# A pair of key chunks gets its maximum from one chunk's scores and a positive score difference, with seven PSUM banks split 4 + 3

## The chip, the core and the metric

The kernel runs on one core of one Trainium2 chip. Its time is the device time of a run in microseconds (us); lower is better. The engines named below are PE (TensorE, the matrix multiplier; PEld is its weight load), DVE (VectorE), ACT (ScalarE), POOL (GpSimd) and SP (SyncE, which issues most transfers). PSUM, where PE writes its results, has eight banks of 128 x 512 float32.

## The reference

Two attention blocks over the same input, each with its own weights, mixed by a gate. There are 2048 tokens, 512 channels and 32 heads of 16 channels, so 64 heads in all.

```python
def _A_ref(x, wqkv, wo):                      # _B_ref is the same
    qkv = ((x @ wqkv).reshape(B, S, 3, H, Dh)).transpose(2, 0, 3, 1, 4)
    q, k, v = qkv[0], qkv[1], qkv[2]
    scores = jnp.einsum("bhqd,bhkd->bhqk", q, k) * (Dh ** -0.5)
    p = _softmax(scores, axis=-1)
    o = jnp.einsum("bhqk,bhkd->bhqd", p, v)
    return o.transpose(0, 2, 1, 3).reshape(B, S, D) @ wo

g = _sigmoid((x * gate_w).sum(-1, keepdims=True))
return g * a + (1 - g) * b
```

The softmax needs, for each query, the maximum of its scores over all 2048 keys.

## The kernel before

**Layout.** q and k are split in two parts each (a rounded one and the rest) and stacked along the rows, 48 rows for a head (`q_st`, `k_st`, three buffers each, one for a head), so that one matmul of 48 rows gives nearly exact float32 scores. The stack stands twice, at rows 0 and 64 (`HALVES`), and `rows()` takes the two in turn, so that two such matmuls run side by side. Two more rows hold the negative maximum of each query.

**Two products for each score.** For a block of 128 queries (a round `m`; 16 rounds are a head, `NT`), `max_product` multiplies the block with the four chunks of 512 keys, and DVE reduces the results over the keys to a maximum. Later, `score` multiplies in the other orientation (128 keys by 512 queries), with the maximum already subtracted by the two added rows; ACT takes exp from PSUM into `p`. `attend` multiplies `p` with V into the bank `acc`, four 32-column groups of PE side by side.

**Loop.** After a prologue (projections of q, k and v, and the maxima of the first 20 rounds, `run_ahead`) the main loop does two rounds a step: eight `score` products for rounds r and r+1, eight products to the maximum for the rounds 20 ahead, and the V product of the rounds before. I call such a step a pair. The engines work through their own queues in order, and the order is written by hand in the string `FULL`, one letter a step: "e" is a `score` with its exp, "m", "A", "B", "x" are the products to the maximum in their order (chunks 0 to 3 of the first round, then of the second), and a digit n stands for `attend_next(n)`, the V product of n quarters (of 128 queries) of a round, four quarters a round. Output projections that are due go in front of the first digit. `LATE` serves the last 10 pairs, whose maxima are all done.

**PSUM and the maximum.** Chunks 0 and 1 go to one bank each out of two (`ps_m1`), chunks 2 and 3 to a double bank (`ps_m2`), which DVE reduces in one go (128x1024). Chunk 1 of the second round of a pair ("x") isn't reduced by DVE directly: ACT copies it to SBUF, POOL takes the maximum of its two halves in three operations (subtract; clamp to at least 0; add), and DVE reduces the remaining 256 columns ("y", a pair later). This is not done for the last block of a head. Three partial maxima a block go to `mxp`; `max_split` joins them once a head, and `max_rows` transposes them (DVE) and sends them through DRAM into the stacks of q. `ps_st` has three banks for the scores, and `acc` one.

**A pool's buffers** are handed out in turn: a product that takes a buffer waits until the last reader of that buffer's former content is done.

Of the kernel before, what the change touches and what calls it, by code (L numbers as in the profile page):

```python
# [51 lines left out]
def gated_mha(ctx: ExitStack, tc: tile.TileContext, xT, x, wqkv_a, wo_a, wqkv_b, wo_b, gate_w, out):  # L52
# [12 lines left out]
    kd = [[dram.tile([2, HG, DH, S], F32, name=f"kd{s}{g}") for g in range(NG)] for s in range(2)]  # L65
    vd = [dram.tile([S, H * 17], F32, name=f"vd{s}") for s in range(2)]
    od = [dram.tile([HG, NQ, 32, 512], F32, name=f"od{g}") for g in range(2 * NG)]
    md = [dram.tile([2, S], F32, name=f"md{i}") for i in range(3)]
# [1 line left out]

    ident = const.tile([P, P], BF, name="ident")
    make_identity(nc, ident)
    q_st, k_st = [], []

    def new_stack(tp):
        i = len(q_st)
# [2 lines left out]
        for b in HALVES:  # L79
            pool.memset(k_st[i][b + 32:b + 64, :].bitcast(F32), -1.0)  # L80

    for _ in range(2):
        new_stack(const)


    def load_stacks(h, halves=HALVES):
# [4 lines left out]
        qs, ks = qd[s][g], kd[s][g]  # L91

        def pairs(t, step):
            v = t[0, j]
            return bass.AP(tensor=v.tensor, offset=v.offset, ap=[[S, DH], [step, 2], [1, S]])
# [11 lines left out]
    PARTS = ((0,), (1,), (2, 3))  # L107
    mxp = {}
    turn = [0]
    banks_m, halved = {}, []  # L110

    def rows():
        turn[0] ^= 1
        return HALVES[1 - turn[0]]

    def max_product(m, c, fold=False):
        h, t = divmod(m, NT)
        if t == 0 and c == 0:
            mxp[h] = small.tile([P, NT, 3], F32, name="mxp")
        q, k = q_st[h % 3], k_st[h % 3]  # L120
        part = min(c, 2)
        if c < 3:
            n = len(PARTS[part])
            banks_m[m] = (ps_m1 if n == 1 else ps_m2).tile([P, n * 512], F32, name=f"ps_m{n}")
        ps = banks_m[m]
        b = rows()
        o = max(0, c - 2) * 512
        pe.matmul(ps[:, o:o + 512], q[b:b + SC, t * P:(t + 1) * P], k[b:b + SC, c * 512:(c + 1) * 512],  # L128
                  start=True, stop=True)
        if fold:  # L130
            x = small.tile([P, 512], F32, name="fold", bufs=2)
            d = x[:, :256]
            act.copy(x, ps)  # L133
            pool.tensor_tensor(d, d, x[:, 256:], op=ALU.subtract)  # L134
            pool.tensor_scalar(d, d, 3.4028234e38, 0.0, op0=ALU.min, op1=ALU.max)  # L135
            pool.tensor_tensor(d, d, x[:, 256:], op=ALU.add)  # L136
            halved.append((mxp[h][:, t, part:part + 1], d))
        elif c != 2:
            dve.tensor_reduce(mxp[h][:, t, part:part + 1], ps, op=ALU.max, axis=AX.X)  # L139

    def max_part(m, part):
        for c in PARTS[part]:
            max_product(m, c)

    def max_halved():
        o, d = halved.pop(0)
        dve.tensor_reduce(o, d, op=ALU.max, axis=AX.X)  # L147

    mparts = {}

    def max_split(h):
        halves = mxp.pop(h)
        m = small.tile([P, NT], F32, name="mrow")
        mp = small.tile([P, 2, NT], F32R, name="mparts")
        dve.tensor_reduce(m, halves, op=ALU.max, axis=AX.X)  # L157
# [25 lines left out]
    with tc.tile_pool(name="xs", bufs=1) as xs, tc.tile_pool(name="pro", bufs=2) as pro, \  # L183
# [34 lines left out]
        def project_qk(s, g, isk, between):  # L218
            hi, lo = wblocks.pop((s, isk * DM + g * P))
            dst = (kd if isk else qd)[s][g]  # L220
            for half in range(2):
                ps = ps_pro.tile([P, 1024], F32, name="ps_pro")
                for c in range(2):
                    cc = half * 2 + c
                    n = 0
                    for a, b in ((hi, xh[cc]), (lo, xh[cc]), (hi, xl[cc])):
                        for k in range(KC):
                            pe.matmul(ps[:, c * 512:(c + 1) * 512], a[:, k], b[:, k],  # L228
                                      start=n == 0, stop=n == 3 * KC - 1)
                            n += 1  # L230
                pt = [pro.tile([P, 1024], F32R, name=f"part{i}") for i in range(2)]
                act.copy(pt[0], ps)  # L232
                dve.tensor_tensor(pt[1], ps, pt[0].bitcast(F32), op=ALU.subtract)  # L233
                for i in range(2):
                    nc.sync.dma_start(dst[i].rearrange("h d t -> (h d) t")[:, half * 1024:(half + 1) * 1024],
                                      pt[i].bitcast(F32))
                between()

        v_st = [const.tile([P, H, 17], F32, name=f"v_st{i}") for i in range(2)]
# [3 lines left out]
        def project_v(s, t):  # L243
            hi, lo = wblocks[s, 2 * DM]
            c, o = divmod(t * P, 512)
            last = s == 1 and t == NT - 1
            ps = ps_m1.tile([P, 512], F32, name="ps_m1") if last else ps_pro.tile([P, 1024], F32, name="ps_pro")
# [24 lines left out]
        ahead = [(m, part) for m in range(NT + LEAD) for part in range(3)]  # L272

        def run_ahead(n):
            turn[0] = 0
            for _ in range(n):
                m, part = ahead.pop(0)
                max_part(m, part)
                if (m, part) == (NT - 1, 2):
# [20 lines left out]
        for t in range(NT):  # L300
            project_v(1, t)
            if pending:
                pending[0] += 1
                if pending[0] == 3:
                    max_rows(pending.pop() - 3)
            if t and t != NT - 2:
                run_ahead(3)
# [120 lines left out]
    banks, fill_only = [], []  # L428

    def result_bank():  # L430
        banks.append(len(banks) % 5)
        if banks[-1] % 2 or not fill_only:
            return ps_m1.tile([P, 512], F32, name="ps_m1")
        return ps_st.tile([P, 512], F32, name="ps_st")

    def project_out(side, t):
# [118 lines left out]
    def attend(r, qa, qb):  # L555
# [13 lines left out]
        if final and last:  # L569
            ev = work.tile([P, 512], F32, name="ev")  # L570
            act.copy(ev, acc)
            hi = work.tile([P, 512], F32R, name="ev_hi")
# [33 lines left out]

    FULL = "eem4emeAeB2emex2AyeB"
    LATE = "ee2ee2ee2ee2"  # L610
    after = {}

    for r in range(0, ROUNDS, 2):
# [8 lines left out]
        if kt == 0 and h + 2 < NH:  # L622
            load_stacks(h + 2)
        m = r + NT + LEAD
        scored = parts = 0
        waiting = len(halved)
        for step in FULL if m < ROUNDS else LATE:
            if step == "e":
                score(r + scored // 4, scored % 4)
                scored += 1  # L630
            elif step in "mABx":
                mm, c = m + parts // 4, parts % 4
                max_product(mm, c, step == "x" and mm % NT != NT - 1)
                parts += 1
            elif step == "y":
                if waiting:
                    max_halved()
            else:
                for a in projects:
                    project_out(*a)  # L640
# [39 lines left out]
```

## Time and profile before

| | |
|---|---|
| Median of 3 runs | 2844.58 us (2844.14 to 2844.75) |
| Profiled execution, span | 2843.0 us |
| Main loop, first exp to end | about 295 to 2812 us |
| Busy share in 900 to 1000 us | PE 98.4%, DVE 95.9%, ACT 95.7%, POOL 35.3% |
| Granted clock of PE there | 1.00 |

The busy share of an engine is the time in which at least one of its instructions is under way; instructions of one engine overlap a little, so the time from one start to the next tells more than the length of one. An entry "[0.42 <-DVE mxp L139]" is idle time of the engine before the instruction and what ended it. In a group's row stand its count, busy time, mean length in ns, and the idle time in front with its releasers.

### The profile page before, as it was taken

To read this page: it belongs to the slowest core of one execution; us is meant where nothing else is said; L and a number is where in the kernel's file an instruction comes from. 1 tells how busy PE (TensorE), PEld (TensorE's weight loads), DVE (VectorE), ACT (ScalarE), POOL (GpSimd) and SP (SyncE) were. 2 spreads that over 40 slices of the span, in tenths; PEclk is the share of its full clock that TensorE was granted. 3 is DMA by queue.
4 is the path that set the end of the run, shared out by engine and by line. 5 is a ranking of instruction groups with operands and counts; after the bars stand their busy time and mean duration, and the time that the engine had idled before them with its cause. 6 is when DMAs were issued, how large, how long until landed. Compare 5 with 4: busy or idle time off the path is not lost.

```text
span 2843.0 us, 56787 instructions
## 1 busy us (share of the span) xinstructions
PE 2795.6 (98%) x22168; PEld 1230.1 (43%) x22168; DVE 2464.7 (87%) x3367; ACT 2412.5 (85%) x4696; POOL 1042.4 (37%) x1686
## 2 busy tenths in 40 slices
PE   8999999999999999999999999999999999999999
PEld 6877433333333333333333444433333333334445
DVE  3135899999999999999999988899999999998884
ACT  3221799999999999999999877899999999998785
POOL 1000355453433333333433555333333344345431
PEclk9999999999999999999999999999999999999999
DMA  6673333222332222232432342232222233233302
GB/s 237 203 229 122 82 69 78 58 52 54 66 58 55 55 43 58 52 56 54 85 54 52 92 94 62 54 56 51 60 43 56 54 70 70 54 72 80 76 6 91
DMA packets 83747, 214.30 MB, mean 75 GB/s; under 512 B 21878, under 2 KB 32086, under 8 KB 70934
## 3 DMA queue, kind: packets, MB, share of 16 engines
q1 hardware_dynamic: 80918, 201.76, 31.2%
q0 software_dynamic: 2560, 8.91, 1.3%
q8 instruction: 174, 2.85, 0.4%
q14 instruction: 95, 0.78, 0.1%
HBM read 145.87 MB, written 64.74 MB: 74 GB/s over the span
## 4 chain that ended last, share of the span: by engine, by line
PE 74%; DVE 16%; ACT 8%; issue 2%; DMA 0%; SPq 0%; ACTq 0%
PE acc L563 28%; PE ps_st L602 22%; DVE mxp L139 14%; PE ps_m L128 12%; PE ps_pro L228 6%; ACT p L604 5%; PE ps_m L445 3%; PE ps_pro L251 3%; ACT ev L580 1%; ACT fold L133 1%; DVE mxp L147 1%; DMA raw<-in_xT 0%; DVE mrow L157 0%; PE ps_st L445 0%; DVE rn L400 0%
## 5 line engine op out<-in xcount | busy, mean ns | idle before, releaser
L139 DVE TENSOR_REDUCE mxp<-ps_m 128x1 f32<-128x512 f32 (+1 forms) x2633 | 2190.3, 890 | 135.1 <-PE ps_m L128 61.0
L604 ACT ACTIVATE p<-ps_st 128x512 f32<-128x512 f32 x4096 | 2153.5, 610 | 177.0 <-PE ps_m L128 100.5
L128 PE MATMUL ps_m<-k_st,q_st 48*128 48x512 f32 x4096 | 1407.2, 441 | 5.3 <-DVE mxp L139 0.8
L602 PE MATMUL ps_st<-q_st,k_st 50*128 50x512 f32 x4096 | 1379.8, 438 | 0.0
L563 PE MATMUL acc<-p,vg 128*17 128x256 f32 (+1 forms) x12360 | 1182.8, 455 | 29.5 <-ACT ev L580 28.0
L602 PEld LDWEIGHTS ps_st<-q_st,k_st 50*128 50x128 f32 x4096 | 662.1, 184 | 801.6 <-ACT p L604 748.0
L128 PEld LDWEIGHTS ps_m<-k_st,q_st 48*128 48x128 f32 x4096 | 677.1, 184 | 251.8 <-DVE mxp L139 233.0
L134 POOL TENSOR_TENSOR fold<-fold 128x256 f32<-128x256 f32 x439 | 321.1, 731 | 1096.5 <-ACT fold L133 1096.5
L563 PEld LDWEIGHTS acc<-p,vg 128*17 128x17 f32 x12360 | 205.3, 95 | 466.3 <-issue 414.6
L136 POOL TENSOR_TENSOR fold<-fold 128x256 f32<-128x256 f32 x439 | 322.1, 734 | 36.6
L133 ACT COPY fold<-ps_m 128x512 f32<-128x512 f32 x439 | 261.3, 595 | 0.0
L135 POOL TENSOR_SCALAR fold<-fold 128x256 f32<-128x256 f32 x439 | 175.6, 400 | 38.5
L147 DVE TENSOR_REDUCE mxp<-fold 128x1 f32<-128x256 f32 x439 | 179.5, 409 | 0.0
L158 POOL CAST mparts<-mrow 128x16 fp32r<-128x16 f32 x64 | 12.6, 197 | 401.0 <-DVE mrow L157 401.0
L232 ACT CAST part<-ps_pro 128x1024 fp32r<-128x1024 f32 x32 | 32.5, 1015 | 132.9 <-PE ps_pro L228 132.9
L233 DVE TENSOR_TENSOR part<-ps_pro,part 128x1024 fp32r<-128x1024 f32 x32 | 39.2, 1225 | 111.4 <-ACT part L232 111.4
L445 PE MATMUL ps_m<-wo,ot 128*128 128x512 f32 (+1 forms) x354 | 90.9, 401 | 0.0
L254 ACT COPY v_st<-ps_pro 128x512 f32<-128x512 f32 x31 | 18.2, 587 | 77.4 <-PE ps_pro L251 77.4
L228 PE MATMUL ps_pro<-xh,whi 128*128 128x512 f32 x256 | 73.0, 404 | 8.8 <-ACT xh L214 8.7
L180 POOL DMA_DIRECT2D vg<-vd x32 | 25.6, 799 | 137.5 <-DMA vd<-v_st 137.1
L445 PEld LDWEIGHTS ps_m<-wo,ot 128*128 128x128 f32 (+1 forms) x354 | 63.9, 188 | 21.3 <-ACT fold L133 7.0
L228 PE MATMUL ps_pro<-xh,wlo 128*128 128x512 f32 x256 | 69.7, 395 | 0.0
(94 smaller groups left out, 822.1 us busy)
## 6 DMA issues: line engine op xcount, KB each, us to landing
k_st<-kd SPq DMA_DIRECT2D x128, 256.0 KB
q_st<-qd SPq DMA_DIRECT2D x128, 256.0 KB
qd<-part SPq DMA_DIRECT2D x32, 512.0 KB
kd<-part SPq DMA_DIRECT2D x32, 512.0 KB
k_st<-kd SPq DMA_DIRECT2D x128, 128.0 KB
q_st<-qd SPq DMA_DIRECT2D x128, 128.0 KB
od<-ev SPq DMA_DIRECT2D x63, 256.0 KB
vd<-v_st SPq DMA_DIRECT2D x32, 272.0 KB
```

The source lines that it names most:

```text
L128: pe.matmul(ps[:, o:o + 512], q[b:b + SC, t * P:(t + 1) * P], k[b:b + SC, c * 512:(c + 1) * 512], start=True, stop=True)
L133: act.copy(x, ps)
L134: pool.tensor_tensor(d, d, x[:, 256:], op=ALU.subtract)
L135: pool.tensor_scalar(d, d, 3.4028234e38, 0.0, op0=ALU.min, op1=ALU.max)
L136: pool.tensor_tensor(d, d, x[:, 256:], op=ALU.add)
L139: dve.tensor_reduce(mxp[h][:, t, part:part + 1], ps, op=ALU.max, axis=AX.X)
L147: dve.tensor_reduce(o, d, op=ALU.max, axis=AX.X)
L228: pe.matmul(ps[:, c * 512:(c + 1) * 512], a[:, k], b[:, k], start=n == 0, stop=n == 3 * KC - 1)
L445: pe.matmul(ps, ot[a][:n, slot, sl], wt[b][:n, g], start=G == groups[0] and i == 0, stop=G == groups[-1] and i == 2)
L563: pe.matmul(acc[32 * c:32 * c + 17, qa * P:qb * P], v[:, 4 * a + c if final else kt, j], p[:, c * 512 + qa * P:c * 512 + qb * P], start=fi ...
L602: pe.matmul(ps, k[b:b + SC + 2, kk * P:(kk + 1) * P], q[b:b + SC + 2, cc * 512:(cc + 1) * 512], start=True, stop=True)
L604: act.activation(pt[r][:, c * 512:(c + 1) * 512], ps, AF.Exp, scale=SCALE)
```

## The change

A maximum of two chunks is taken as max(s0, s1) = s0 + max(s1 - s0, 0). Since scores are linear in k, s1 - s0 is the product of q with the difference of the two key chunks. The prologue makes that difference for each head (`rise_k`: one DVE and three POOL operations in each of eight blocks, and two more writes to DRAM), `load_stacks` loads it into `x_st` (48 rows by 512; two more loads a head).

For the first round of each pair (from the first pair whose products can be made ahead) chunks 0 and 1 are then done in two steps. "D" (`max_rise`), a pair earlier: a product with `x_st`, and ACT writes its positive part (Relu) to SBUF. "A" (`max_pair`): a product with chunk 0, and one DVE operation adds the positive part and takes the maximum over the 512 columns. All other chunks are plain 512-column reductions ("m", `max_plain`): six a pair. ACT's copies, POOL's halving and the double bank are gone; `mxp` has four columns a block, the unused one preset to the lowest number by POOL. The number of PE products is the same. `ps_m` has three banks for all products to the maximum, and `ps_st` four. The order of a pair is new, and the V product is cut 3, 3 and 2 quarters instead of 4, 2 and 2; the second 3 is the last quarter of one round and two of the next.

```diff
-    ps_m1 = ctx.enter_context(tc.tile_pool(name="ps_m1", bufs=2, space=PSUM))
-    ps_m2 = ctx.enter_context(tc.tile_pool(name="ps_m2", bufs=1, space=PSUM))
+    ps_m = ctx.enter_context(tc.tile_pool(name="ps_m", bufs=3, space=PSUM))
...
+        if h and halves[-1] == HALVES[1]:
+            x = x_st[h % 2]
+            dma(x[:32].bitcast(F32), pairs(xs, HG * DH * 512, 512))
+            dma(x[32:SC].bitcast(F32), xs[0, j])
...
-    def max_product(m, c, fold=False):
+    def scores_bank(m, c):
         h, t = divmod(m, NT)
...
+        ps = ps_m.tile([P, 512], F32, name="ps_m")
         b = rows()
...
+        pe.matmul(ps, q[b:b + SC, t * P:(t + 1) * P], k, start=True, stop=True)
+        return ps, mxp[h][:, t]
+
+    def max_plain(m, c):
+        ps, o = scores_bank(m, c)
+        dve.tensor_reduce(o[:, c:c + 1], ps, op=ALU.max, axis=AX.X)
...
+    def max_rise(m):
+        ps, _ = scores_bank(m, "rise")
+        rises[m] = small.tile([P, 512], F32, name="rise")
+        act.activation(rises[m], ps, AF.Relu)
+
+    def max_pair(m):
+        ps, o = scores_bank(m, 0)
+        rise = rises.pop(m)
+        dve.tensor_tensor_reduce(out=rise, in0=ps, in1=rise, scale=1.0, scalar=LOWEST,
+                                 op0=ALU.add, op1=ALU.max, accum_out=o[:, 0:1])
...
+                if isk and half == 0:
+                    d = pro.tile([P, 512], F32, name="rise_k", bufs=1)
+                    dve.tensor_tensor(d, ps[:, 512:], pt[0][:, :512].bitcast(F32), op=ALU.subtract)
+                    pool.tensor_tensor(d, d, pt[1][:, :512].bitcast(F32), op=ALU.subtract)
+                    dt = [pro.tile([P, 512], F32R, name=f"rise_p{i}", bufs=1) for i in range(2)]
+                    pool.tensor_copy(dt[0], d)
+                    pool.tensor_tensor(dt[1], d, dt[0].bitcast(F32), op=ALU.subtract)
+                    for i in range(2):
+                        nc.sync.dma_start(xd[s][g][i].rearrange("h d t -> (h d) t"), dt[i].bitcast(F32))
...
-            project_qk(s, g, isk, lambda: run_ahead((i >= 10) + (i >= 13)))
+            project_qk(s, g, isk, run_ahead if i >= 10 else lambda: None)
...
-    ps_st = ctx.enter_context(tc.tile_pool(name="ps_st", bufs=3, space=PSUM))
+    ps_st = ctx.enter_context(tc.tile_pool(name="ps_st", bufs=4, space=PSUM))
...
-    FULL = "eem4emeAeB2emex2AyeB"
-    LATE = "ee2ee2ee2ee2"
+    FULL = "m3memeem3meAe2Dmeee"
+    LATE = "e2ee2ee2ee2e"
...
+            elif step == "m":
+                max_plain(*plain.pop(0))
+            elif step == "D":
+                if m + 2 < ROUNDS:
+                    max_rise(m + 2)
+            elif step == "A":
+                if m in rises:
+                    max_pair(m)
+                else:
+                    max_plain(m, 0)
+                    max_plain(m, 1)
```

**PE's queue.** One pair in the middle of a head before, from its 512-column V product on (`ps_m` is the maximum's bank, of either kind; `[waits ...]` names the engine whose progress the instruction waits for):

```order
L563 MATMUL acc<-p,vg 17x512 x4
L602 MATMUL ps_st<-q_st_2010,k_st_2011 128x512 [waits Activation_49]
L128 MATMUL ps_m_12733<-k_st_114,q_st_113 128x512
L602 MATMUL ps_st<-q_st_2010,k_st_2011 128x512 [waits Activation_49]
L128 MATMUL ps_m_12739<-k_st_114,q_st_113 128x512 [waits DVE_49]
L602 MATMUL ps_st<-q_st_2010,k_st_2011 128x512 [waits Activation_49]
L128 MATMUL ps_m_12739<-k_st_114,q_st_113 128x512
L563 MATMUL acc<-p,vg 17x256 x4
```

The same place after the change, from "D" of one pair to the second V product of the next:

```order
L135 MATMUL ps_m<-x_st_127,q_st_123 128x512 [waits DVE_49]
L135 MATMUL ps_m<-k_st_124,q_st_123 128x512 [waits DVE_49]
L615 MATMUL ps_st<-q_st_2132,k_st_2133 128x512 [waits Activation_49] x3
L135 MATMUL ps_m<-k_st_124,q_st_123 128x512 [waits DVE_49]
L576 MATMUL acc<-p,vg 17x384 x4
L135 MATMUL ps_m<-k_st_124,q_st_123 128x512 [waits Activation_49]
L615 MATMUL ps_st<-q_st_2132,k_st_2133 128x512
L135 MATMUL ps_m<-k_st_124,q_st_123 128x512 [waits DVE_49]
L615 MATMUL ps_st<-q_st_2132,k_st_2133 128x512 [waits Activation_49] x2
L135 MATMUL ps_m<-k_st_124,q_st_123 128x512 [waits DVE_49]
L576 MATMUL acc<-p,vg 17x128 x4
L576 MATMUL acc<-p,vg 17x256 x3
```

Three products to the maximum now stand in one group with three scores between two V products, each in a bank of its own with a wait of its own, where two of three shared a double bank and one wait.

**DVE's queue.** One pair before (L139 reduces 512 or 1024 columns, L147 the halved 256):

```order
L139 TENSOR_REDUCE mxp<-ps_m_11268 128x1
L139 TENSOR_REDUCE mxp<-ps_m_11283 128x1
L139 TENSOR_REDUCE mxp<-ps_m_11293 128x1
L139 TENSOR_REDUCE mxp<-ps_m_11299 128x1
L139 TENSOR_REDUCE mxp<-ps_m_11314 128x1
L147 TENSOR_REDUCE mxp<-fold 128x1
```

And after (L140 reduces 512 columns; L152 is the add with its maximum, in two instructions):

```order
L140 TENSOR_REDUCE mxp_7708<-ps_m_8091 128x1
L140 TENSOR_REDUCE mxp_7708<-ps_m_8098 128x1
L140 TENSOR_REDUCE mxp_7708<-ps_m_8105 128x1
L140 TENSOR_REDUCE mxp_7708<-ps_m_8114 128x1
L140 TENSOR_REDUCE mxp_7708<-ps_m_8125 128x1
L152 ISA rise_8077,mxp_7708<-ps_m_8131,rise_8077 128x512
L152 ISA mxp_7708 128x1
L140 TENSOR_REDUCE mxp_7708<-ps_m_8146 128x1
```

Six instructions a pair became eight, seven of which read 512 columns of PSUM.

More of the change, by code (lines that the diff above doesn't have):

```diff
@@ L60, in gated_mha @@
     dram = ctx.enter_context(tc.tile_pool(name="dram", bufs=1, space=DRAM))
-    ps_m1 = ctx.enter_context(tc.tile_pool(name="ps_m1", bufs=2, space=PSUM))
-    ps_m2 = ctx.enter_context(tc.tile_pool(name="ps_m2", bufs=1, space=PSUM))
+    ps_m = ctx.enter_context(tc.tile_pool(name="ps_m", bufs=3, space=PSUM))
     qd = [[dram.tile([2, HG, DH, S], F32, name=f"qd{s}{g}") for g in range(NG)] for s in range(2)]
     kd = [[dram.tile([2, HG, DH, S], F32, name=f"kd{s}{g}") for g in range(NG)] for s in range(2)]
+    xd = [[dram.tile([2, HG, DH, 512], F32, name=f"xd{s}{g}") for g in range(NG)] for s in range(2)]
     vd = [dram.tile([S, H * 17], F32, name=f"vd{s}") for s in range(2)]
@@ L72, in gated_mha @@
     make_identity(nc, ident)
-    q_st, k_st = [], []
+    q_st, k_st, x_st = [], [], []
     def new_stack(tp):
@@ L80, in new_stack @@
             pool.memset(k_st[i][b + 32:b + 64, :].bitcast(F32), -1.0)
-    for _ in range(2):
+    for i in range(2):
         new_stack(const)
+        x_st.append(const.tile([SC, 512], F32R, name=f"x_st{i}"))
     def load_stacks(h, halves=HALVES):
@@ L90, in load_stacks, with pairs @@
         q, k = q_st[h % 3], k_st[h % 3]
-        qs, ks = qd[s][g], kd[s][g]
-        def pairs(t, step):
+        qs, ks, xs = qd[s][g], kd[s][g], xd[s][g]
+        def pairs(t, step, n=S):
             v = t[0, j]
-            return bass.AP(tensor=v.tensor, offset=v.offset, ap=[[S, DH], [step, 2], [1, S]])
+            return bass.AP(tensor=v.tensor, offset=v.offset, ap=[[n, DH], [step, 2], [1, n]])
         for b in halves:
@@ L114, in rows @@
         return HALVES[1 - turn[0]]
-    def max_product(m, c, fold=False):
+    def scores_bank(m, c):
         h, t = divmod(m, NT)
[L118 to L125, printed above, removed]
-        b = rows()
[L127 to L147, printed above, removed]
+        if h not in mxp:
+            mxp[h] = small.tile([P, NT, 4], F32, name="mxp")
+            if h:
+                pool.memset(mxp[h][:, FIRST % NT if h == 1 else 0::2, 1:2], LOWEST)
+        ps = ps_m.tile([P, 512], F32, name="ps_m")
+        b = rows()
+        q = q_st[h % 3]
+        if c == "rise":
+            assert b == 0
+            k = x_st[h % 2][:]
+        else:
+            k = k_st[h % 3][b:b + SC, c * 512:(c + 1) * 512]
@@ L151, in gated_mha @@
     mparts = {}
     def max_split(h):
-        halves = mxp.pop(h)
+        parts = mxp.pop(h)
         m = small.tile([P, NT], F32, name="mrow")
         mp = small.tile([P, 2, NT], F32R, name="mparts")
-        dve.tensor_reduce(m, halves, op=ALU.max, axis=AX.X)
+        dve.tensor_reduce(m, parts, op=ALU.max, axis=AX.X)
         pool.tensor_copy(mp[:, 0], m)
@@ L236, in project_qk @@
                                       pt[i].bitcast(F32))
+                if isk and half == 0:
[5 more added lines that the diff above has]
+                    pool.tensor_tensor(dt[1], d, dt[0].bitcast(F32), op=ALU.subtract)
+                    for i in range(2):
+                        nc.sync.dma_start(xd[s][g][i].rearrange("h d t -> (h d) t"), dt[i].bitcast(F32))
                 between()
@@ L246, in project_v @@
             last = s == 1 and t == NT - 1
-            ps = ps_m1.tile([P, 512], F32, name="ps_m1") if last else ps_pro.tile([P, 1024], F32, name="ps_pro")
+            ps = ps_m.tile([P, 512], F32, name="ps_m") if last else ps_pro.tile([P, 1024], F32, name="ps_pro")
             n = 0
@@ L271, in gated_mha, with run_ahead @@
                 block(load_w, c)
-        ahead = [(m, part) for m in range(NT + LEAD) for part in range(3)]
-        def run_ahead(n):
+        ahead = [(m, c) for m in range(NT + LEAD) for c in range(4)]
+        def run_ahead():
             turn[0] = 0
[L276 to L279, printed above, removed]
+            for _ in range(min(3, len(ahead))):
+                m, c = ahead.pop(0)
+                max_plain(m, c)
+                if (m, c) == (NT - 1, 3):
                     max_split(0)
@@ L305, in gated_mha @@
                     max_rows(pending.pop() - 3)
-            if t and t != NT - 2:
-                run_ahead(3)
+            if t:
+                run_ahead()
         assert not ahead and not pending
@@ L430, in result_bank @@
     def result_bank():
-        banks.append(len(banks) % 5)
+        banks.append(len(banks) % 7)
         if banks[-1] % 2 or not fill_only:
-            return ps_m1.tile([P, 512], F32, name="ps_m1")
+            return ps_m.tile([P, 512], F32, name="ps_m")
         return ps_st.tile([P, 512], F32, name="ps_st")
@@ L571, in attend @@
             act.copy(ev, acc)
-            hi = work.tile([P, 512], F32R, name="ev_hi")
+            hi = work.tile([P, 512], F32R, name="ev_hi", tag="num")
             lo = work.tile([P, 512], F32R, name="ev_lo")
@@ L624, in gated_mha @@
         m = r + NT + LEAD
-        scored = parts = 0
-        waiting = len(halved)
+        plain = [(m, 2), (m, 3)] + [(m + 1, c) for c in range(4)]
+        scored = 0
         for step in FULL if m < ROUNDS else LATE:
@@ L630, in gated_mha @@
                 scored += 1
[L631 to L637, printed above, removed]
+            elif step == "m":
[6 more added lines that the diff above has]
+                    max_pair(m)
+                else:
+                    max_plain(m, 0)
+                    max_plain(m, 1)
             else:
```

6 lines of the change are left out of this document (3 added, 3 removed).

## The prediction

> **What bounds the kernel now.** I read the page first, for its span and its chain of waits.
>
> ```profile
> span 2843.0 us, 56787 instructions
> PE 2795.6 (98%) x22168; PEld 1230.1 (43%) x22168; DVE 2464.7 (87%) x3367; ACT 2412.5 (85%) x4696; POOL 1042.4 (37%) x1686
> PE 74%; DVE 16%; ACT 8%; issue 2%; DMA 0%; SPq 0%; ACTq 0%
> ```
>
> No DMA stands on the chain; TensorE has three quarters of it and VectorE most of the rest. Almost all of the span is the main loop: 512 pairs of rounds, of which 502 still make score products for a maximum (the last 10 run LATE), and 32 of the 502 carry an output projection. One head is eight pairs, and one transposition of maxima (L164) is done per head, so the view of that tile gives the time of a head:
>
> ```profile
> L164 DVE STREAM_TRANSPOSE mt<-mparts x3: 200/202/202, 1017.3 to 1093.2; 128x32 f32<-128x32 f32 x3
> ```
>
> Three of them are two heads apart from first to last: 75.9 us, 37.95 us a head, 4.74 us a pair. Next, the timeline of TensorE over one pair (start, duration, engine, line, what). Score products for the softmax are L602, those for the maximum L128, two of which run side by side in two halves of the rows; L563 is the product with V.
>
> ```profile
> 1004.10 1.05 PE L563 MATMUL acc<-p,vg 128*17 128x512 f32 x8
> 1005.08 0.49 PE L602 MATMUL ps_st<-q_st,k_st 50*128 50x512 f32 x1
> ...
> 1005.41 0.40 PE L602 MATMUL ps_st<-q_st,k_st 50*128 50x512 f32 x1
> ...
> 1005.65 0.46 PE L602 MATMUL ps_st<-q_st,k_st 50*128 50x512 f32 x1
> ...
> 1006.04 0.62 PE L563 MATMUL acc<-p,vg 128*17 128x256 f32 x8
> 1006.60 0.49 PE L602 MATMUL ps_st<-q_st,k_st 50*128 50x512 f32 x1
> ...
> 1006.94 0.39 PE L602 MATMUL ps_st<-q_st,k_st 50*128 50x512 f32 x1
> ...
> 1007.27 0.63 PE L563 MATMUL acc<-p,vg 128*17 128x256 f32 x8
> 1007.82 0.49 PE L128 MATMUL ps_m<-k_st,q_st 48*128 48x512 f32 x1
> ...
> 1008.16 0.39 PE L128 MATMUL ps_m<-k_st,q_st 48*128 48x512 f32 x1
> ...
> 1008.40 0.40 PE L128 MATMUL ps_m<-k_st,q_st 48*128 48x512 f32 x1
> 1008.73 0.62 PE L563 MATMUL acc<-p,vg 128*17 128x512 f32 x4
> ```
>
> From start to start: a V product of 512 columns holds TensorE for 0.98 us, one of 256 for 0.56; a first couple of score products is followed by the second after 0.33, the second by the third after 0.23, and the last by the V product after 0.33. That adds to 4.63 us, and nothing in it is a hole: in a pair with a folded chunk TensorE itself sets the period. VectorE is as good as full beside it:
>
> ```profile
> 1006.31 1.21 DVE L139 TENSOR_REDUCE mxp<-ps_m 128x1 f32<-128x1024 f32 x1
> 1007.44 0.68 DVE L139 TENSOR_REDUCE mxp<-ps_m 128x1 f32<-128x512 f32 x1
> 1008.04 0.41 DVE L147 TENSOR_REDUCE mxp<-fold 128x1 f32<-128x256 f32 x1
> 1008.59 4.75 DVE L139 TENSOR_REDUCE mxp<-ps_m 128x1 f32<-128x1024 f32 x6
> ```
>
> Reductions follow each other faster than they last: one of 1024 after 1.13 us, one of 512 after 0.60. The one at 1008.59 had to wait for its product at 1008.16, so a result can be read 0.43 us after the product starts. Three of 512, two of 1024 and the 256 one (0.33, from 1013.25 to 1013.58 below) are 4.39 us of a 4.62 us pair. What makes the mean 4.74 are the pairs around a head's end, without a fold and with the copy of acc.
>
> **The change part by part.** *Removed.* 439 ScalarE copies, GpSimd's three operations on each, and 439 reductions of 256. GpSimd's work is behind no one here, and costs nothing now or later.
>
> ```profile
> L139 DVE TENSOR_REDUCE mxp<-ps_m 128x1 f32<-128x512 f32 x1609 | 1057.9, 680 | 70.4 <-PE ps_m L128 55.8 <-PE ps_st L602 11.0
> L604 ACT ACTIVATE p<-ps_st 128x512 f32<-128x512 f32 x4096 | 2153.5, 610 | 177.0 <-PE ps_m L128 100.5 <-PE ps_st L602 53.0
> L133 ACT COPY fold<-ps_m 128x512 f32<-128x512 f32 x439 | 261.3, 595 | 0.0
> L233 DVE TENSOR_TENSOR part<-ps_pro,part 128x1024 fp32r<-128x1024 f32 x32 | 39.2, 1225 | 111.4 <-ACT part L232 111.4
> L202 DVE TENSOR_TENSOR wlo<-wraw,whi 128x512 fp32r<-128x512 f32 x16 | 10.9, 683 | 46.9 <-ACT whi L201 46.9
> L451 DVE SCALAR_TENSOR_TENSOR o_acc<-ps_m,gate,o_acc 128x512 f32<-128x512 f32 x22 | 16.5, 751 | 9.8 <-PE ps_m L445 9.8
> ```
>
> *Added on ScalarE.* A Relu of 128x512 out of PSUM in every pair; I take it as the copy that it replaces (595 ns; exp, 610 ns, is the other bound). ScalarE is not full and keeps its place.
>
> *Added on VectorE.* Six reductions of 512 a pair instead of three of 512 and two of 1024, and one fused add-and-maximum, which the built program holds as two instructions: the main one, and one that only writes the maximum to 128x1. The trace has neither. For the main one the nearest rows are the two-input operations: 683 ns for 512 elements (L202) and 1225 for 1024 from PSUM (L233), as long as the plain reduction, and 751 (L451) with a scalar besides. How soon the next can follow, and what a tiny instruction takes, these rows show:
>
> ```profile
> 2821.29 0.75 DVE L451 SCALAR_TENSOR_TENSOR o_acc<-ps_st,gate,o_acc 128x512 f32<-128x512 f32 x1
> 2821.98 0.75 DVE L451 SCALAR_TENSOR_TENSOR o_acc<-ps_m,gate,o_acc 128x512 f32<-128x512 f32 x1
> ...
> 1013.25 0.41 DVE L147 TENSOR_REDUCE mxp<-fold 128x1 f32<-128x256 f32 x1
> 1013.58 1.22 DVE L139 TENSOR_REDUCE mxp<-ps_m 128x1 f32<-128x1024 f32 x1
> 1014.83 0.20 DVE L157 TENSOR_REDUCE mrow<-mxp 128x16 f32<-128x48 f32 x1
> 1014.95 0.68 DVE L139 TENSOR_REDUCE mxp<-ps_m 128x1 f32<-128x512 f32 x1
> ```
>
> So the main one lets the next start after 0.60 (plain reduction) to 0.69 us; I take 0.63, near the reduction, since it needs no scalar from memory. The small one lasts 0.20 us and blocks for 0.12. VectorE's work in a pair is then 6 x 0.60 + 0.63 + 0.12 = 4.35 us against 4.39: the change takes next to nothing off VectorE. In the pairs without a fold it saves some.
>
> *Moved, and the wait that it makes.* This is the term that decides. Write a pair's step string as m1 |3| m2 e m3 e e m4 |3| m5 e A e |2| D m6 e e e. All eight products to the maximum now take their PSUM bank from one ring of three, so each waits until the one three before it has been read: m2 for D's Relu, m3 for m6, m4 for m1, m5 for m2, A for m3, D for m4, m6 for m5, and **the next pair's m1 for A**, and there for its second instruction, which alone signals. VectorE reads in order m1 to m5, A, m6. Behind the waiting m1 stand, on TensorE's queue, the V product and then m2, m3 and m4, on which VectorE waits next. That closes a loop through both engines:
>
> From m1 to the V product, 0.33 us. The V product of 384 columns: 0.98 and 0.56 are 0.42 apart for 256 columns, so half-way between them, 0.77. From there m2 starts a group; its couple is followed after 0.33 rather than 0.23, so it truly begins 0.10 late, and its result is there after 0.43 + 0.10 = 0.53. VectorE starts on m2 at 1.63. m3 and m4 come 0.33 and 0.56 behind m2, and behind m4 the next V product: it starts at 1.10 + 0.56 + 0.33 = 1.99, takes 0.77 (or 0.91 if its two pieces, of 128 and 256 columns, pay the fixed 0.14 twice), and m5's result is there at 3.29 to 3.43, when VectorE needs it (1.63 + 3 x 0.60). So it runs m2, m3, m4, m5 without a hole, 4 x 0.60, and starts A at 4.03. A's signal comes with the end of the small instruction, 0.63 + 0.20 = 0.83 later, at 4.86. From a release to the product:
>
> ```profile
> 1003.97 1.23 DVE L139 TENSOR_REDUCE mxp<-ps_m 128x1 f32<-128x1024 f32 x1
> ...
> 1005.25 0.18 PEld L128 LDWEIGHTS ps_m<-k_st,q_st 48*128 48x128 f32 x1
> ...
> 1005.42 0.40 PE L128 MATMUL ps_m<-k_st,q_st 48*128 48x512 f32 x1
> ```
>
> The reduction ends at 1005.20, the weights load from 1005.25 and the product starts at 1005.42: 0.22 at most, as it was also behind its forerunner; I take 0.20. The next m1 starts at **5.06 us**. TensorE alone would bring it after 4.6 to 4.75 us (the old flow, and up to 0.14 for the V product in two pieces); VectorE alone needs 4.35, and sits idle between m1's result and m2's, while TensorE multiplies with V. Before, with two buffers of 512 and a wide one of 1024, the waits' view has 558 loads that VectorE released, 0.42 us each in the mean and the length of a gap behind a V product, and TensorE's rows above have no hole:
>
> ```profile
> PEld ps_m L128 <- DVE mxp L139: 233.0, 558, 0.8
> PE acc L563 <- ACT ev L580: 28.0, 62, 0.5
> ```
>
> The transposition between m4 and m5 adds 0.12 once a head. The copy of acc, on which TensorE waits 0.45 us a head now, is covered by the longer loop. A pair is thus 5.06 + 0.02 = 5.08 against 4.74 us.
>
> *Covered.* Three reductions of 512 behind a block of the projections, the difference of key chunks (one VectorE operation of 0.68 us, three on an idle GpSimd) and 16 more writes lie under 24 projection matmuls; each write holds SP's queue until GpSimd is done, and behind it stand writes that are due a half block later. Without that cover, eight times some 3 us would show. Two more loads a head (96 KB) on SP come five pairs before their use. LATE gets a fourth bank for exp: 0 to 5 us less over ten pairs, I take 2. In a pair with projections, which are slow pairs now already, I take 0.15 more instead of 0.34, between nothing and that: 5 us for the 32.
>
> *Sum.* 470 x (5.08 - 4.74) = 160, + 5 - 2 = 163 on the span of 2843.0: 3006. The three runs have a median of 2844.58, 1.6 above the profiled span, so **3007 us** (an error of 0.01 us in the loop is 5 us of it).
>
> [...]
>
> **The rivals.** *TensorE's own flow decides, and it gets faster.* If A's bank came free before TensorE reaches m1, at about 4.6 us of the pair, the old 4.62 would hold in every pair and the slow pairs of a head would go: 502 x 0.12 = 60 us less, 2785. The signal from A would have to come within 4.62 - 0.20 - 4.03 = 0.39 us of its start; a plain reduction of 512 blocks for 0.60. Or the V product would have to be no part of the loop, but TensorE takes its queue in order. For it speaks that no engine gets more work. Chance 0.06.
>
> [...] Chance 0.04.
>
> *The prologue shows.* If GpSimd's three operations, some 3 us, stood in the way in each of eight blocks, 25 us come on top, 3029. TensorE is never idle there now. Chance 0.04.
>
> **How the numbers follow.** The forecast has 0.86. Its own bounds: the fused operation's signal after 0.75 (0.60 and 0.15) and release 0.17 give 4.95, that is 55 less; the signal after 0.95 (0.75 end to end and 0.20) and release 0.22 give 5.20, 70 more. With 10 us for the rest the range is 2938 to 3078, which takes in the prologue's case. A change under 0.2%, 6 us, could not be told from none. Faster is the first rival with little else: 0.05; a loop between the two that happens to meet 4.74 is 0.02; slower 0.93.
>
> **What would show it.** In the profile after, pairs of 5.0 to 5.1 us, 40.5 us from one transposition to the next; waits of the weight load of m1 for the fused line, some 500 of them of a few tenths each; VectorE idle before m2's reduction for some 0.5 us in each pair; ScalarE's busy share down. Wrong would be a pair of 4.6 us with TensorE still gapless, a fused row of over 1.1 us, or a small instruction far from 0.2 us.

## The result, and the profile after

| | before | after |
|---|---|---|
| Median | 2844.36 us (2843.87 to 2844.75) | 2918.16 us (2917.25 to 2919.01) |
| Profiled execution, span | 2843.0 us | 2916.6 us |

The change makes the kernel slower: 1.026 times the time before, with a 95% interval of 1.0246 to 1.0274, which is 74 us. The forecast was 163 us.

Where the time went is read from the transposition of maxima, done once for each of the 64 heads. These are the rows of that tile over the whole run, the first from the kernel before (count, shortest, median and longest ns, first and last start):

```profile
L164 DVE STREAM_TRANSPOSE mt<-mparts x64: 199/201/213, 288.6 to 2768.8; 128x32 f32<-128x32 f32 x64
```

and the second from the changed kernel:

```profile
L168 DVE STREAM_TRANSPOSE mt<-mparts x64: 199/200/211, 290.7 to 2842.7; 128x32 f32<-128x32 f32 x64
```

Up to the first of them the change costs 2.1 us. From the first to the last it costs 71.8 us (2552.0 against 2480.2), and from the last to the end of the span nothing (73.9 against 74.2). That is 71.8 / 63 = 1.14 us a head, 0.14 a pair. It is spread over the whole loop: from the 2nd transposition to the last, each head loses between 0.4 and 1.7 us. In the stretch that the prediction read, a pair now takes 39.1 / 8 = 4.89 us, against 4.74:

```profile
L168 DVE STREAM_TRANSPOSE mt<-mparts x3: 201/202/202, 1001.9 to 1080.1; 128x32 f32<-128x32 f32 x3
```

From the page of the changed kernel, with its rows for the new VectorE operation and for the reductions:

```profile
span 2916.6 us, 65382 instructions
PE 2898.3 (99%) x26176; PEld 1417.1 (49%) x26176; DVE 2392.9 (82%) x4399; ACT 2497.8 (86%) x4758; POOL 255.0 (9%) x456
PE 97%; DMA 1%; ACT 1%; DVE 0%; issue 0%; SPq 0%; DVEq 0%
L152 DVE CUSTOM_DVE_ANT_0 rise<-ps_m,rise 128x512 f32<-128x512 f32 x501 | 339.9, 678 | 0.0
L140 DVE TENSOR_REDUCE mxp<-ps_m 128x1 f32<-128x512 f32 x3094 | 1956.7, 684 | 261.1 <-PE ps_st L615 190.7
```

VectorE has lost 72 us of work and idles 261 us ahead of its reductions (the row names the score product that starts side by side with the product waited for; in the pair below m2 and that score both start at 1004.52). The chain of waits gives TensorE 97% of the path and the second row calls it 99% busy. Taken alone this would say that TensorE has no time to spare. The waits say something else. These two rows of the whole run are weight loads of products to the maximum that stood until VectorE had read their bank (us in total, times, longest):

```profile
PEld ps_m L135 <- DVE mxp L140: 404.0, 955, 1.3
PEld ps_m L135 <- DVE mxp L152: 126.5, 490, 0.3
```

The first row's waits are 0.42 us each in the mean. In the pair below they are the loads of m5 and D, which come right behind a V product, and 0.42 us is as long as that V product holds TensorE by itself once its own weights are loaded: from the V product of 256 columns at 1006.85 to D's product at 1007.41 it is 0.56 us, as it was before the change (1006.04 to 1006.60), and its loads take the first 0.13. The second is the one that matters: 490 times, once in nearly every one of the 502 pairs, a load waits for the fused operation L152. One pair shows where. First TensorE, from the next pair's m1 of one pair to that of the following one (start, duration, what):

```profile
1003.32 0.50 PE L135 MATMUL ps_m<-k_st,q_st 48*128 48x512 f32 x1
1003.75 0.84 PE L576 MATMUL acc<-p,vg 128*17 128x384 f32 x8
1004.52 0.50 PE L135 MATMUL ps_m<-k_st,q_st 48*128 48x512 f32 x1
...
1008.20 0.49 PE L135 MATMUL ps_m<-k_st,q_st 48*128 48x512 f32 x1
```

Then VectorE in the same stretch:

```profile
1003.24 1.30 DVE L140 TENSOR_REDUCE mxp<-ps_m 128x1 f32<-128x512 f32 x2
1005.05 2.48 DVE L140 TENSOR_REDUCE mxp<-ps_m 128x1 f32<-128x512 f32 x4 [0.51 <-PE ps_m L135]
1007.45 0.68 DVE L152 CUSTOM_DVE_ANT_0 rise<-ps_m,rise 128x512 f32<-128x512 f32 x1
1008.06 0.08 DVE L152 DVE_READ_ACCUMULATOR2_ANT mxp<- 128x1 f32 x1
```

And the weight load that closes the circle:

```profile
1008.19 0.18 PEld L135 LDWEIGHTS ps_m<-k_st,q_st 48*128 48x128 f32 x1 [0.26 <-DVE mxp L152]
```

Read in turn: m1 starts at 1003.32, the V product behind it at 1003.75, and m2 behind that at 1004.52. VectorE, idle for 0.51 us, starts on m2 at 1005.05, reduces m2 to m5 without a hole, and starts A at 1007.45. A's small instruction, which writes the maximum, ends at 1008.14, and the next m1 starts at 1008.20, 4.88 us after the last. That is the whole period. Neither engine is full; each waits once a pair for the other.

### The profile page after: what moved, and what is told of

Same layout as the page of the kernel before. It is cut to its first block, busy times and chain, and to the rows that moved or that the text cites. A ratio compares the mean times of both kernels' runs of the same rounds, so it can differ in the third digit from the quotient of the medians.

```text
span 2916.6 us, 65382 instructions
## 1 busy us (share of the span) xinstructions
PE 2898.3 (99%) x26176; PEld 1417.1 (49%) x26176; DVE 2392.9 (82%) x4399; ACT 2497.8 (86%) x4758; POOL 255.0 (9%) x456
## 4 chain that ended last, share of the span: by engine, by line
PE 97%; DMA 1%; ACT 1%; DVE 0%; issue 0%; SPq 0%; DVEq 0%
PE ps_m L135 39%; PE acc L576 37%; PE ps_st L615 10%; PE ps_pro L232 5%; PE ps_m L458 3%; PE ps_pro L264 3%; ACT p L617 1%; DMA raw<-in_xT 0%; DMA k_st<-kd 0%; DMA qd<-part 0%; PE ps_st L458 0%; PE ps_st L509 0%; DVE mxp L140 0%; PE ps_m L509 0%; DVE part L237 0%
## 5 line engine op out<-in xcount | busy, mean ns | idle before, releaser
L617 ACT ACTIVATE p<-ps_st 128x512 f32<-128x512 f32 x4096 | 2153.7, 606 | 118.0 <-PE ps_st L615 84.5
L140 DVE TENSOR_REDUCE mxp<-ps_m 128x1 f32<-128x512 f32 x3094 | 1956.7, 684 | 261.1 <-PE ps_st L615 190.7
L576 PE MATMUL acc<-p,vg 128*17 128x384 f32 (+1 forms) x16368 | 1186.2, 384 | 2.9 <-ACT ev L584 2.0
L615 PE MATMUL ps_st<-q_st,k_st 50*128 50x512 f32 x4096 | 1187.4, 421 | 0.0
L135 PEld LDWEIGHTS ps_m<-k_st,q_st 48*128 48x128 f32 x3595 | 616.1, 184 | 690.3 <-ACT p L617 298.2
L576 PEld LDWEIGHTS acc<-p,vg 128*17 128x17 f32 x16368 | 314.8, 96 | 455.2 <-issue 435.6
L152 DVE CUSTOM_DVE_ANT_0 rise<-ps_m,rise 128x512 f32<-128x512 f32 x501 | 339.9, 678 | 0.0
L147 ACT ACTIVATE rise<-ps_m 128x512 f32<-128x512 f32 x501 | 301.5, 602 | 42.4 <-PE ps_m L135 0.3
L135 PE MATMUL ps_m<-x_st,q_st 48*128 48x512 f32 x501 | 249.4, 498 | 0.0
L135 PEld LDWEIGHTS ps_m<-x_st,q_st 48*128 48x128 f32 x501 | 91.7, 183 | 212.3 <-DVE mxp L140 183.8
L232 PE MATMUL ps_pro<-xl,whi 128*128 128x512 f32 x256 | 69.0, 391 | 0.0
```

The costliest lines, as they stand in the source:

```text
L135: pe.matmul(ps, q[b:b + SC, t * P:(t + 1) * P], k, start=True, stop=True)
L140: dve.tensor_reduce(o[:, c:c + 1], ps, op=ALU.max, axis=AX.X)
L147: act.activation(rises[m], ps, AF.Relu)
L152: dve.tensor_tensor_reduce(out=rise, in0=ps, in1=rise, scale=1.0, scalar=LOWEST, op0=ALU.add, op1=ALU.max, accum_out=o[:, 0:1])
L232: pe.matmul(ps[:, c * 512:(c + 1) * 512], a[:, k], b[:, k], start=n == 0, stop=n == 3 * KC - 1)
L576: pe.matmul(acc[32 * c:32 * c + 17, qa * P:qb * P], v[:, 4 * a + c if final else kt, j], p[:, c * 512 + qa * P:c * 512 + qb * P], start=fi ...
```

## The experiments

All edits are to the changed kernel. The kernel before, run beside them, took 2844.83 and 2844.86 us in the two groups of runs. In a pair's string, m, A and D are products to the maximum, e is a score with its exp, and a digit is so many quarters of V products. The products to the maximum are called m1 to m6, A and D, in the prediction's order.

**Out of the ring.** D's product takes its bank from the four of the scores. ScalarE reads that bank, as it reads the scores' banks. Seven products, not eight, are left for the ring of three. The bank three back from the next m1 is then m5's; it is m2, behind the V product, that waits for A.

```diff
-        ps = ps_m.tile([P, 512], F32, name="ps_m")
+        ps = ps_st.tile([P, 512], F32, name="ps_st") if c == "rise" else ps_m.tile([P, 512], F32, name="ps_m")
```

> D's product takes a score bank (of four) instead of one of the ring of three; all else as after the change. Loop theory: the next m1 then waits for m5's reduction instead of for the fused A, which comes 0.67 us earlier, the loop is cut, and a pair falls from 4.87 to what TensorE alone needs, 4.55 to 4.65 us: some 110 to 160 us less than after the change, 2760 to 2810, faster than before. Rival, TensorE's own flow is 4.87 us (the V product cut in two pieces): no change, 2918. Rival, VectorE's work with the fused operation sets the pair: no change either, since VectorE does the same.

It took 2805.71 us (2803.92 to 2806.38), 0.9864 times the kernel before (0.9849 to 0.9878): 112 us less than the changed kernel, and 39 less than the kernel before, as expected of the loop. The engines execute the same instructions, with the same counts; one line takes away the loss and more. Of the 490 loads that waited for A none is left in the ring's products; the 16 that still wait for it belong to output projections. A head in the same stretch takes (1080.5 - 1006.0) / 2 = 37.25 us, 4.66 a pair:

```profile
L168 DVE STREAM_TRANSPOSE mt<-mparts x3: 200/200/201, 1006.0 to 1080.5; 128x32 f32<-128x32 f32 x3
```

Its V products behind m1 show two pairs, of 4.58 and 4.62 us:

```profile
1002.86 0.84 PE L576 MATMUL acc<-p,vg 128*17 128x384 f32 x8
1007.44 0.84 PE L576 MATMUL acc<-p,vg 128*17 128x384 f32 x8
1012.06 0.84 PE L576 MATMUL acc<-p,vg 128*17 128x384 f32 x8
```

**A longer V product inside the loop.** The V product between m1 and m2 gets four quarters, the next one two. The columns multiplied are the same, but no piece runs across two rounds any more, so TensorE has 4008 matmul instructions fewer (22168, as many as before the change, against 26176).

```diff
-    FULL = "m3memeem3meAe2Dmeee"
+    FULL = "m4memeem2meAe2Dmeee"
```

> V product cut 4, 2, 2 as before the change: 512 columns between m1 and m2, and no piece across two rounds, so TensorE has one call less. Loop theory: 0.21 us longer, 5.08 us a pair, 107 us more, 3025. Rival, TensorE's flow with the piece cut in two: faster than 2918 by up to 0.14 x 502 = 70 us, 2848.

It took 3026.55 us (3025.52 to 3028.76; ratio 1.064, 1.0622 to 1.0658). The expectation of the loop was met to 2 us. TensorE's rows show the longer term itself, 0.99 us from the V product to m2 (1005.26 to 1006.25) where it had been 0.77:

```profile
1004.84 0.50 PE L135 MATMUL ps_m<-k_st,q_st 48*128 48x512 f32 x1
1005.26 1.05 PE L576 MATMUL acc<-p,vg 128*17 128x512 f32 x8
1006.25 0.49 PE L135 MATMUL ps_m<-k_st,q_st 48*128 48x512 f32 x1
```

0.22 us in 502 pairs is 110 us; 108 were measured. TensorE multiplies the same columns in fewer instructions, so more work is not what makes the kernel longer; and if the piece cut in two set the time, the kernel would have become faster.

**A shorter V product inside the loop.** The same the other way, two quarters between m1 and m2, three in each of the others.

```diff
-    FULL = "m3memeem3meAe2Dmeee"
+    FULL = "m2memeem3meAe3Dmeee"
```

> V product cut 2, 3, 3 instead of 3, 3, 2: the piece between m1 and m2 is 256 columns instead of 384; the work is the same. Loop theory: the loop is 0.21 us shorter, 4.66 us, 502 x 0.21 = 105 us less, 2813; if the scores behind that piece then wait for their banks, up to 4.78, 2870. Rivals (TensorE's flow, VectorE's work): the sum over the pair is the same, so 2918.

It took 2888.1 us (2887.44 to 2889.1; ratio 1.0155, 1.014 to 1.017), only 30 us less, and outside what was expected. With 0.56 (1005.56 to 1006.12) for 0.77 us the loop's own sum is 4.67 us a pair; the heads in the trace give (1071.1 - 1032.6) / 8 = 4.81.

```profile
L168 DVE STREAM_TRANSPOSE mt<-mparts x2: 200/200/201, 1032.6 to 1071.1; 128x32 f32<-128x32 f32 x2
```

The trace shows another wait in the loop's place. A score of the second group waits for the exp that empties its bank:

```profile
1006.92 0.18 PEld L615 LDWEIGHTS ps_st<-q_st,k_st 50*128 50x128 f32 x1 [0.31 <-ACT p L617]
```

In the stretch from 900 to 1100 us there are 42 such waits in this run, one a pair, of 0.3 us:

```profile
PEld ps_st L615 <- ACT p L617: 12.9, 42, 0.3
```

against five in the changed kernel:

```profile
PEld ps_st L615 <- ACT p L617: 0.8, 5, 0.2
```

This wait is part of a second loop, through ScalarE, whose other half the trace shows as well: D's Relu stands ahead of the exps on ScalarE's queue, and ScalarE idles until D's product comes.

```profile
1010.10 0.60 ACT L147 ACTIVATE rise<-ps_m 128x512 f32<-128x512 f32 x1 [0.29 <-PE ps_m L135]
```

Once round: the load of that score at 1006.92, a V product at 1007.35 and another at 1008.79, D's product at 1009.56, its Relu at 1010.10, two exps behind it of which the second ends at 1011.67, and the load of the same score of the next pair at 1011.72. That is 4.80 us, the period of the pair. In the stretch from 900 to 1100 us ScalarE waits so 36 times:

```profile
ACT rise L147 <- PE ps_m L135: 10.3, 36, 0.3
```

That this second loop is what holds the pair at 4.81 us is read from the rows; no run took it away alone.

**Is it the fused operation?** A becomes a plain maximum over the same 512 columns, at the same place of the order. Chunk 1 of those rounds is left out of the maximum.

```diff
-        dve.tensor_tensor_reduce(out=rise, in0=ps, in1=rise, scale=1.0, scalar=LOWEST,
-                                 op0=ALU.add, op1=ALU.max, accum_out=o[:, 0:1])
+        dve.tensor_reduce(o[:, 0:1], ps, op=ALU.max, axis=AX.X)
```

> A is a plain reduction of chunk 0 instead of the fused addition and maximum: the positive part is made and not used, so chunk 1 is left out of the maximum of one round in two. Loop theory: a plain reduction signals 0.68 us after its start as the two fused instructions together do (0.69), so within 6 us of 2918. Rival, the fused operation is what the change costs: 2850 or less.

It took 2913.71 us (2912.72 to 2916.46; ratio 1.0246, 1.0231 to 1.0261), 4 us less than the changed kernel. The operation's row in this run:

```profile
L152 DVE TENSOR_REDUCE mxp<-ps_m 128x1 f32<-128x512 f32 x501 | 340.0, 679 | 0.0
```

The plain operation lasts 679 ns; the fused one with its small instruction lasts 0.69 us (1007.45 to 1008.14). So of the 74 us, 4 to 5 are due to what the new operation is; the other 69 stay with a plain operation at the same place of the loop.

**One more VectorE operation, inside the loop and outside.** A reduction of 256 columns that nobody uses is added once a pair, either between m5 and A (inside) or between m1 and m2, where VectorE idles (outside). It reads SBUF and takes no bank.

```diff
+    extra = const.tile([P, 1], F32, name="extra")
...
+    def max_extra():
+        dve.tensor_reduce(extra, v_st[0].rearrange("p h d -> p (h d)")[:, :256], op=ALU.max, axis=AX.X)
...
-    FULL = "m3memeem3meAe2Dmeee"
+    FULL = "m3memeem3mezAe2Dmeee"
...
+            elif step == "z":
+                max_extra()
```

> One more VectorE reduction in each of 502 pairs, of 256 columns of a table in SBUF that nobody reads, queued between m5 and A, so on the loop. Such a reduction (the halved chunk before the change) blocked VectorE for 0.33 us. Loop theory: A starts 0.33 us later, 502 x 0.33 = 165 us more than after the change, 3083. Rival, TensorE's own flow sets the pair: VectorE has some 0.6 us idle a pair, so 2918.

The second kernel differs from it in the place of z alone:

```diff
-    FULL = "m3memeem3mezAe2Dmeee"
+    FULL = "mz3memeem3meAe2Dmeee"
```

> The same reduction, as often, queued between m1 and m2, where VectorE idles while TensorE multiplies with V. Loop theory: hidden, 2918 within 10 us. Rival, the sum of VectorE's work sets the pair: as much more as the other one, 3083.

Inside it took 3082.1 us (3081.37 to 3082.27; ratio 1.0835, 1.0816 to 1.0853), 164 more; outside 2924.05 us (2923.53 to 2924.64; ratio 1.028, 1.0265 to 1.0295), 6 more. Both as the loop has it. In the first, A starts 0.32 us later than the extra operation:

```profile
1007.52 0.41 DVE L116 TENSOR_REDUCE extra<-v_st 128x1 f32<-128x256 f32 x1
1007.84 0.68 DVE L157 CUSTOM_DVE_ANT_0 rise<-ps_m,rise 128x512 f32<-128x512 f32 x1
```

and 0.32 x 502 is 161 us. It comes back in the waits of m1's load for A, over the whole run:

```profile
PEld ps_m L140 <- DVE mxp L157: 284.8, 485, 0.6
```

which is 158 us more than the 126.5 of the changed kernel, while in the second kernel the same row has not moved:

```profile
PEld ps_m L140 <- DVE mxp L157: 127.2, 484, 0.3
```

**Four banks for the maximum, three for the scores.** The ring that makes the wait gets a bank from the other.

```diff
-    ps_m = ctx.enter_context(tc.tile_pool(name="ps_m", bufs=3, space=PSUM))
+    ps_m = ctx.enter_context(tc.tile_pool(name="ps_m", bufs=4, space=PSUM))
...
-    ps_st = ctx.enter_context(tc.tile_pool(name="ps_st", bufs=4, space=PSUM))
+    ps_st = ctx.enter_context(tc.tile_pool(name="ps_st", bufs=3, space=PSUM))
```

> PSUM split the other way: four banks in the ring of the maximum's products, three for the scores. The next m1 then waits for m5, so the loop through A is cut as with D in a score bank. If the ring of three alone were the cost: 2800 to 2850. Second theory, which the run with the V product cut 2, 3, 3 suggests: with three score banks the third score of the second group waits for an exp of the group before, which now closes a loop through ScalarE; then no faster than 2918, up to 3000.

It took 3018.22 us (3017.66 to 3018.9; ratio 1.0611, 1.0595 to 1.0627), 100 us more than the changed kernel and 18 above the upper figure expected. The loop through A is cut here too: in the stretch from 900 to 1100 us no load waits for A, where 40 did in the changed kernel. But the ring of the scores now makes TensorE wait: 112 times in 200 us, more than two a pair, where there were five.

```profile
PEld ps_st L615 <- ACT p L617: 26.1, 112, 0.3
```

As with the shorter V product, this is a reading of the waits; how the 100 us are made up was not taken apart.

**What is left without the loop.** The first kernel again, with D in a score bank, and the order of the letters changed so that a score stands ahead of the V product and the seventh product to the maximum at the end.

```diff
-    FULL = "m3memeem3meAe2Dmeee"
+    FULL = "e3memeem3meAe2Dmeem"
```

> D in a score bank, and m1 moved behind the last score of its couple (FULL e3memeem3meAe2Dmeem). If the waits of that couple for exp still cost time in the version with D in a score bank: 5 to 15 us less than 2806. If TensorE's own work is all that is left: 2806 within 4.

It took 2803.0 us (2802.5 to 2804.58; ratio 0.9855, 0.984 to 0.987), 2.7 less than the first, whose runs go from 2803.92 to 2806.38 us, and within the 4 us expected if TensorE's own work is all that is left. The waits of the scores' loads for exps have halved over the whole run (the first row is the first kernel's, the second this one's), yet the time fell by 2.7 us alone:

```profile
PEld ps_st L615 <- ACT p L617: 179.2, 861, 0.4
PEld ps_st L615 <- ACT p L617: 91.4, 443, 0.4
```

## Why the prediction was right or wrong

**Right: the mechanism.** The forecast said slower, because m1 would wait for A's second instruction with the V product and m2 to m4 queued behind it, while VectorE sits idle for some 0.5 us ahead of m2. The trace has each of these: 490 waits of m1's load for A, and 0.51 us of idle time. The runs show that this loop sets the time. 0.22 us added to its V product costs 108 us and 0.32 us added to its VectorE part costs 164, each in full; the same operation outside it costs 6; and one line that opens the loop gives 112 back.

**Wrong: the size of the term "A's signal".** The forecast's sum of 5.06 us, against the rows of the pair shown above:

| term | forecast | measured | from |
|---|---|---|---|
| release to m1 | 0.20 | 0.06 | 1008.14 to 1008.20 |
| m1 to V product | 0.33 | 0.43 | 1003.32 to 1003.75 |
| V product | 0.77 | 0.77 | to 1004.52 |
| m2's result | 0.53 | 0.53 | to 1005.05 |
| m2 to m5 | 2.40 | 2.40 | to 1007.45 |
| A's signal | 0.83 | 0.69 | to 1008.14 |
| sum | 5.06 | 4.88 | |

Three terms were met to 0.01 us. The first two differ in how the time is cut between them, for here the record of m1 starts with its weight load (1008.19) and in the row that the prediction read it started behind it; together they are 0.49 instead of 0.53. What failed is the last, 0.14 of the 0.18 us: the prediction gave the small instruction 0.20 us, the length of a small reduction (L157 of the kernel before), and the accumulator read takes 82 ns. It named a small instruction far from 0.2 us as a sign that the step would be wrong, and it was. The lower bound failed with it: 0.75 us for the signal rested on 0.15 for the small instruction. An operation with no row in the trace was held to be hardly shorter than the short reductions there. 0.18 us in the 470 pairs that the forecast counted are 85 of the 89 us between 3007 and 2918. The ends of the range, 2938 and 3078, are not what the terms named for them add up to: 55 and 10 less than 3007 are 2942, 70 and 10 more are 3087. The measured time lies below either lower end.

**The other terms.** The prologue's extra work stays hidden, as said: 2.1 us up to the first transposition, not the 25 of the rival. The new operation takes 678 ns (a plain reduction of 512 columns 684), so the fused row of over 1.1 us that would have shown the step to be wrong did not come: no run shows a slower fused operation, for which a chance of 0.04 stood. ScalarE's busy share was to go down and went up, from 85 to 86% of a longer span. The exps take as much as before (2153.7 against 2153.5 us), but 501 Relus stand where 439 copies were:

```profile
L617 ACT ACTIVATE p<-ps_st 128x512 f32<-128x512 f32 x4096 | 2153.7, 606 | 118.0 <-PE ps_st L615 84.5 <-PE ps_m L135 7.7 <-DVE mxp L140 1.2
L147 ACT ACTIVATE rise<-ps_m 128x512 f32<-128x512 f32 x501 | 301.5, 602 | 42.4 <-PE ps_m L135 0.3
```

That is 40 us more of Relus (301.5 against 261.3). The rest of the 85 us by which ScalarE's busy time rose is overlap: busy time counts a stretch once however many instructions are under way in it, and in longer pairs less of it is hidden under the next instruction. Between 900 and 1100 us ScalarE is busy for 0.519 us an instruction in the changed kernel (194.23 us, 374 of them), and for 0.500 with the loop cut (196.41 us, 393). The forecast took a Relu in every pair as the copy that it replaces, though 501 stand for 439. Its sum had no term for this, and ScalarE has no part in the loop above.

**The rival of TensorE's own flow** came near to what lies behind the loop. It said that without the wait the old 4.62 us would hold in every pair, 2785 us in all. With the loop cut the two pairs shown take 4.58 and 4.62 us, a head's mean is 4.66 a pair, and the run takes 2805.71. So the change without the loop is worth 39 us against the kernel before, and the loop, closed by the one bank that D takes out of the ring of three, costs 112.

**Open.** With a loop through the score banks and ScalarE's exps I explain why a shorter V product and a fourth bank for the maximum bring less than the first loop alone would allow. Rows show its waits, and with the shorter V product its whole round of 4.80 us; no run changed it by itself. What sets the 4.66 us that are left with both loops open was not taken apart.

## What to carry to other kernels

When tiles read by different engines share one ring of PSUM banks, write down for each product which instruction frees the bank that many places back, and follow the queue behind the one that waits: if the engine that frees the bank needs something from that queue, the circle has a period of its own, and the time can't fall below its sum, however idle both engines look (here 4.88 us a pair, with VectorE busy 82% of the span). Here it was enough to move the one tile that ScalarE reads into the ring of ScalarE's other tiles (2918.16 to 2805.71 us); taking a bank from that ring instead made the kernel slower (3018.22 us), so the check is due for both rings. An instruction that the old trace lacks may be shorter than the small ones in it (82 ns here, against 0.20 us), so let the range reach below the shortest.

## What the runs showed of the hardware that was not expected

The read of the accumulator takes 82 ns and starts 0.61 us after the fused operation does (1007.45 to 1008.06), so the maximum of 512 columns that falls out of the addition is there as soon as that of a plain reduction, 0.69 against 0.68 us. And TensorE's records cover waits: the window from 900 to 1100 us of the changed kernel shows it busy for the whole of the 200 us, with 181 for VectorE, while 40 of its loads, one in nearly every pair, wait for the fused operation there, 10.3 us in all (columns: length, PE, PEld, VectorE, ScalarE, GpSimd, clock, share of DMA, GB/s).

```profile
900.00:1100.00 200.00, 200.00 (x1968) 89.54 (x1968) 181.01 (x340) 194.23 (x374) 4.67 (x18) 1.00 0.32 58
```

The kernel with the loop cut (D in a score bank) shows the same 200.00, and 4.7% more matmuls in it:

```profile
900.00:1100.00 200.00, 200.00 (x2060) 85.15 (x2055) 186.85 (x355) 196.41 (x393) 5.45 (x19) 1.00 0.36 67
```
